# A new written-out order for a five-engine kernel, with one planned duration set from 0.345 to 0.42

## The chip, the cores and the metric

One NeuronCore of a Trainium2 chip (trn2) runs the whole kernel. Its engines are TensorE (PE for matmuls, PEld for its weight loads), VectorE (DVE), ScalarE (ACT), GpSimd (POOL) and SyncE (SP), which issues nearly all DMA transfers. The metric is the device time of one execution in microseconds; smaller is better.

## The reference

Two attentions over the same input `x` (2048 tokens of 512 values) are mixed by a gate.

```python
x = A_x
g = _sigmoid((x * gate_w).sum(-1, keepdims=True))
a = _A_ref(x, A_mem0, A_Wq, A_Wk, A_Wv, A_Wo, A_seg_len)   # recurrent memory, 64 segments
b = _B_ref(x, B_wq, B_wk, B_wv, B_wo, B_beta)              # 4 segments, 32 heads of 16
return g * a + (1 - g) * b
```

The first one is a recurrence. A segment has 8 memory rows and 32 tokens; its output for the memory rows is the memory of the next segment:

```python
for s in range(n_seg):                        # 64 segments of 32 tokens
    h = jnp.concatenate([mem, xs], axis=1)    # 40 rows of 512
    q, k, v = (einsum('btd,dhe->bhte', h, W) for W in (Wq, Wk, Wv))   # 32 heads of 128
    p = softmax(where(mask, q k^T * scale, -1e9))
    o = einsum('bhte,hed->btd', p v, Wo)
    mem = o[:, :M, :]
    outs.append(o[:, M:, :])
```

The second one is an attention within four stretches of 512 tokens, plus a running memory of `phi(k)^T v` over the stretches. It has no recurrence from token to token and so fills the waits of the first.

## The kernel before, in words

The program records some 6,800 operations, each with an engine (or two engines to choose from), what it reads and writes, a planned duration `cost` in microseconds and a priority. `Prog.schedule` then plans: it gives PSUM banks, picks engines and forms of matmuls, and lays down the order on each engine. `Prog.emit` writes the instructions in that order, with semaphore waits for what an operation reads. Each engine works through its own list strictly in order.

In this kernel the order isn't chosen by the planner's priorities. It is written out: the string `ORDER` (lines 15 to 80) holds, for each of the five engines, the sequence of operations, and `sequences()` unpacks it. Where an operation may go to two engines, the list in which it stands decides. With `ORDER` given, the planned durations still set the planned times, and by these the planner gives PSUM banks and orders waits.

```python
words = [a | b << 8 for a, b in zip(raw, raw[len(raw) // 2:])]
for e in self.ENGS:
    ...
    for w in words[at + 1:at + 1 + n]:
        prev += 1 + (w - 65536 if w > 32767 else w)
        out[e].append(self.all[prev])
```

One segment `s` of the first attention (`p_seg`) goes through these steps, for two halves `r` of 16 heads. TensorE's 128 columns are mostly used as four quarters of 32, so that four matmuls with 32-column weights run side by side.

- `k`, `q`, `v`: projections of the 32 rows `hT` (24 tokens and 8 memory rows), line 1422. Each is evicted from PSUM by ScalarE or VectorE (line 1002); k and q are then turned by VectorE (line 1497).
- `H` (line 1029) writes the mask into PSUM, `S` (lines 1512 and 1516) adds the scores, and ScalarE takes the exponential `exp` (line 1521) into `PT`.
- `U` (line 1536): TensorE sums the columns of `PT`. ScalarE takes `ln` (line 1540) and `rc`, the exponential of its negative (line 1542). VectorE multiplies: `nrm` (line 1544). A smaller multiplication `nrr` (line 1546) goes to VectorE or GpSimd.
- `PV` (line 1577) and `PW` (line 1586): probabilities times values, into four PSUM banks, evicted as `OT` by ScalarE or VectorE (line 1002).
- `wo` (line 1314): the output projection. VectorE turns its memory rows, two copies swap blocks, and `hm` (line 1337) writes the memory rows of the next segment's `hT`.

Around these stand the work for the eight rows of each segment that are not on the recurrence (`rk`, `rq`, `rv`, `wor`, done for four segments at once), the second attention (`bL`, its scores, line 1146; `bE`, exponentials, line 1164; `bM`, masks on GpSimd, line 1170; `bPV`, line 1187; `bout`) and the final rows (`brow`, `fin`).

The one planned duration that the change touches stands at line 1545, in `p_u`, which also holds `U`, `ln`, `rc` and `nrr`:

Of the kernel before, what the change touches and what calls it, by code (L numbers as in the profile page):

```python
# [19 lines left out]
    "jybi^^oj}%>U%zo>Jb8OZ<N}L1(=#JDDoS_`pkgh2B0%=U>r|~rbo`cqusO2TW~0a<WCe1=<RUh>xlYGAT@awnt*sMpDAF5er(SIgaCr*VEC!Gp!1GiZ{)5^AJm?7j_+?@1XVC66"  # L20
    "fK}v0dtnjOMt8&ES#TM#+-5CV24f)gF^mT=dd2_h7_tMPi`R}>Q*C+|IKc{F8M+b*CahBw{|@l86F&Jw<gJA$VEhbw5jb2flMdk9=>lxN@wK9KSIXHo05@sWTy_w|B0V@xG|X$k!"
    "5Qc(z>l4d0gO{L*8zySK|+AI=Yc|?i|A>-rv~5b&x$60G`~bF5g;`*UeUgp8#$P~WuO<H3;HrU6qp@?poi!G*1ZFJdo>Z@TR5FXf;4NkN4_;Q_>=tEN6g`@fLb1bpaQZOiBXA>+V"
    "H_fUo0j7tZRV`qWIE%l9QVe4i}WBen=dJJ$-3R$`vD)ECd(}i!6v}wbKMbU|KIybFj0I<yVs21`WWjcz74CIxX<zN6}V_>`=sknfI7Lom-iDQqlY4j3tj35S_u#NIL8@#(|@(^gD"
    "q0MO1`W<fvwgK|q|<WpWYQIAZErNVb+NA!hN)%6Z)m)oCLd#K2<P`G#<>Spirme1+>R!DTrEufjoS2e3LBmW(FSix)!Cv_)X{<k$nW+{BAwE4V<Gi@XNJ6qu-J|I%D~`W1pX(dr6"
    "(Zsdy$M1J#|UcaIjK_A87OP!BGmm~3{MiDW2`b1JS#zG4zYL8z&jn!$w&VgMtAR!PCfvr_vXm#I&D5^58Xr!WX?sD?;Wsu1EGvETU^t@Rm^QJ;WnomV`C2^nywC;mQ$Yfy?Ur|D_"
    "+x^7LIRr4fPb(%|7#Kycye@;J*805BKVblW2D^Y*GHwNd0uQboqwdro;&<wLP(!K-hDODb5;6!@=<%CuNDROMkMxyQ!@7G&;`g2uwoqyYIK2&-U4g}V{#iBP3SzT(=$yDIx0r};d"
    "Nfrr`}5L`NyOOQqQPFs*-F9YE_D=Av!#v~1t^1;Pt@?xMDN{1dK?MP(&QfgfDlfp4L48({ACl!_Z={bdSQl?kBP9gHeF!YDiZ}!fSaJ`F@)>OoG{{7l9QCr;5++xqT}nYJ(f%ef~"
    "c~)u+~#VO0>bU0*1m<2xW-kOk04bH`epzFFYc_HvHD-Ka11iv=>z?H<I=tQX?Qxb~61n`atq8hKl#IxN?r?i*2q4HEG5LAY^gk%flVv+w|Ack1N&eV+-P*$I%~$fqC(V=2F6+_tK"
    "`$8cX!18sAl7csb{#;Jk*=Paxt!Za1~P%cZhXN^zu1U15uA4^8D0gNtMmY~^4ON{QNWB&IM|jnZ6*Xhn-kCz4tQhr7rk=C+VQPuR<@C=B(ynW-%49~@;K9!UNyT@S$JF#tytozt5"
    "C5q%x@h_(LpPy`V@*Acw6w7TY-iq_!{C<tnj^Sg(%r<~diL6o##{=@EL37^jN263L+F9ox%n6xg^Gt&DDu=FUTEBz%LVBu$V;StF#Po6I_Sl#@!P^<e$H^}ZKKyE(N>>^7aeuavs"  # L30
    "k{{#SP{$7ig0u5Y#H#>}Wt<&{zDiRhT?0mtAHBEmPeKPL;WPxrHfu(gCf6ag`T(LL?1@J_fS6ROGaBXcH@L-8_<H^ipOtaX;r-0nFvbWeghvU(DST1;KExcXR$dh9w3HG@%d90<&"
    "ZW<b$c$)3=>3m_l&*Y%8{2^}?JvWB^OX~U;fkSdIUfR$4m;v2B`Bx%y#9>54MH3xB7MT$<H0T`m}T6&coXW6Tz;aqV#X!tpSC9S7t)}gBN}W{riGy>zgB*<TzR7uy-}OUuQyyO)-"
    "siOn$h@AL#ivGJ0EhjT1YoyYvW@MFLY>wp|);&Ib8AT;<D}gmu1TFWeRi2Xv>GoU=hpKt%IM&zyT+LjSMg{%J4pXZF;3H(_mrLFQqV+Mk!eItZb1NzWE}MK`K&_YyvM`A%AvKzYV"
    "6M0H<G6fTl+~AFZw|9zwo$KKdS=2?!i51O%%Fm0IS_mN~K|<SP-X20y3A9NgotFGgo9z#&ED)b^)HyWPWZdZABn)#r-7Kv>_;>|+c47YjIdg`vPoNGMcK=SH8l(t6$@=uwE7Cp>8"
    "J4G5f9fY3Gsdp_1c|2}SxF2o#+IoO!z`7&Dd$OV5rg4fas^_$65>v`>`tO75lLm)1OSd4-&iXHX_h^bH?qYv@SS-tpTj8@=i{0!Fx@dx;B>^y*$&Ibf2aaey?M-8ZvZ+2K906G;w"
    "WHuyZ#$|TBj5~wi3Yz~Vw*NjLKy;YPcpls)v}Wj_Jww``O8;rn?AhSbTfj}M4%p7)QNd<#1yT{P@4!jC%?t&m@28UsI&1?}pF;uNPRSB&F4OJ+^+iK~Symw&j*0|(Ke%>FY#=)BN"
    "0spfp&%?Kz=B6z9)ysf+03461+@^^-o}?i&M^U}c-C+77cFah+fy~TfT9r3H41Qh_k%GH?u0wY8qIIZc3Da0hh!jwt)LdMEzr%qwFd=0Yf$sPLpEI?83~L)1Ja1Ir4Am7O(Z5i7H"
    "sQrz;oYifr9W2n9Nw<l2@YM>RO+vTNqYiL!3<xQL)MTck{vq0&;jvo<Gh^0@8rGT41v2z;L1?*n+3d2;pr7mOweE(dIlIws*&e8XG)n-JF5!io%L><BK7Hv&ktcHjy~mb#d?~jV!"
    "hHj}G5V!QGw)64V9AOABTQzYPI(_@{P9>#MSPW`ymLx8jZ+ez)#j6d+sV=8A(zM$#eqPWZlF9-{?1D%y77{uvWcu*Wk2=1nIHIxroS<Q3gq^AiCitVL6|%S*}&loDNz?@|#Ovrg7"
    "tVs-B{y-BQ})dBi8M82qy(AlnBfoa~TlvstPHxaIbt8p>sJ>DE0b{9e41Ft?THB#-==UG!__3IXK+mmE1QP(Vx{pH-D1WKNm@Fcc2U4-G+QC{ppooCOXH7RU|H$SZ$i`v6)H=-7b"  # L40
    "VYu9TE#oa2e;Z&jsaRW&V{)EovUA||DA8f|LP&=Ln{Y%?&x_<KQD;2W0SBf{m_LaM<h6(5pzs2C2JQ12AqAhbglp-*#);na7n|lyhXr4N4HEHLgWwPD#SSD!HVDR{8{Tu6y*US{T"
    "kwLx);kMarJ>-i{{Z3k#8<PtesK_jfMBE~8$sYcJX(AOU-e^=7McSr$ZHXiS};|I!wb9Pdqj^{>_L5m!wW)1Ls6Lb%H0O&)dMxW-~+*eaNMm3PL2ezgRlUCx~tOTlSM@YAZOAy(+"
    "z^dU-Z??&t7;^!!dagxF)QSuheG>mt@P{{&6k&yP1Anj1uhzysfLXqOsecGwI$Kd#-IvuRHeD@OQnTYhdUyFp@WD)?z{RsFYnxlhNo;lcTNY6C1fJ96$HrHx0|rXq`8t&3>?OYX?"
    "<)v4CH<205=bz9qa^@ie%`w2z&>@rdipAA1>}Y<sNaEnKu|7!KOjkIQ_`aOA`+2z);0%UvJ+8~U&==D!`yqx>Z^gP?-f8^WGLRxBJYiwogJsIWS%SPX(jZ_m)f`L?y(R5c1SxjAF"
    "em3A((TYd)g<DKgO4K}3}ggy+(tB<TAIIyr_ivBEgIMqG7`|tZV8~Nw9D~(7yxX?66;Pox<=z@QIw_#p%1sPj_sQLbL4t`I7jDfJ_Z8&ptNO=pV37awgBQ*N`wG}1~GOjj$hb(@x"
    "$L$wMgZv5_=6w(3`p8ws<7k`RxA?wD+K|&itkvnWA-iuO*&o67enCHF?^!q*%58Z1OtOy7fU|ejn+1Dczju7PY33VEZbgYEJY~*<8jquiU0IN@um83IuqEc;fV9~lbWf`VqK&)Wm"
    "@~|T_g<pj2L%-x!C1<pcE^eLHa#6l!5o)a|8f)IZe0_I*B$SjT>DXlfrGOT6Un`zj+c|WkZq92lVI-X?FktNt3M_87S^#sd~n-hT=Dtxk;_RShz%LNchAa`N5NyA-ii47OK#CbjE"
    "4Rc^wok2GbtuAle8~)ID=&y0*D2I*$(JxvpV<c=QYQ<4LMV6CJM-jDZSOqaN@tjO^FD;T4yG=+*XVo7hj_Jsxx99+TA-Oq<sF@XIoYD%>=UYnHDCl>A8##$O79wD6U_|6HbL$lY)"
    "S+undQd2qO6_jog+ZyNH7X6Sog?C!dI=2Pkl1KD5Wikt?t`I+f<+{ntJs*MsKn${?xgeze#OBK1p$Y84|uV=_#Ue~D%h>OFlQU_Ey*&XzU+-hz>jXE^Uix-A&Fr=~#1b49^Jh$ZB"
    "Kj3fJ@+zZ6kmx~U+wPRvFpyWP1U{ofqun~D`&-jOX!<z3!3Fz{j=<AVtzRDBfac~gS&et0pZaR>l_PUYFY0QSs{%Y$07~WG4=}=;-Nj8(vvuTS#-)wPnpQZHPiQHq>dsF0v*66`$"  # L50
    "81>sk!f}o4=bK;Vih@c{_TEkYK(+s%9xsqdfk*h>+efG&@G)9Cb3sM|ByQTA7#@gc%@N^J;~-8?#`T0Lo%$1vTLwZs&QgZSQ{RpY`Y6R#VSYEYZqj_YZflnF*tB*qiP>jM1v76Lx"
    "E0K`Z#2O-8y9gratC7)%HIur>2P_oH=a5yYQkI;n?VCiEI!?xR{q1S1Ny>01x@Z%OiXc3SV99w9Ex1ok02W&F&$f`osM!Wg6KOHpZqKX7=?>w%-6eOCfSAKok<17?w1P)`fgwR$O"
    "OidduJj~x$o(-yYpW(YG}hZ1SQBsGeG8i?(EC<)WH$&EZ#B^F0=#KIRvhU+i`mD-JdS&pVnU<ev@8sI$U`0Hu3RNGCp5lw!B>5^PH|(F4V5>B1tBS4tKQUb5GF4xmyy)en0m6C^L"
    "3jNYXx8H0~D?+{Dl5Ha}~S>29C%0>$E!NaA?Z-`0R)fMug{-@4h5ApMmSGO65-&=YXcWh49lUDIhYBAoUXO_3paJq+FegHrGO`@W##8=s^L&mYI@_a~fvd~%@<MRqwtTGCrvW#O4"
    "OcF`k%HyT{u9nIsrQ5e;~PQ#rOa}d2jwI}WvyZB=-5PAKlORlF}Jx#rRC-;hxR}h-Kl8g|LU+a~_)f*d2&0=oXoEXlq_ib83)dwy~gctF=X+>6#aOCY~u`A_W07v>I@2ep=-2H&O"
    "=q`ZX0fB@gMUu=D-MM_eR)vKo5;%7?{$a@DFo6324GBNw_8=3q#fdCUAJsOwF0?PQo^3@FX)Mp`gV7N&4jpLm`KC8qU~7}@aF!!8IJqhNr)B<d=E?lIoevt;&dJ@-=MutYoo%5HJ"
    "DeLSX4~&_Vfn2b{J;5Soz5<u>3~MTrsUtsHjMb?)0Z|9YlV<Qo3EViGI>tUcl`93**pH7xO30Ljwk!Zgyl~?b*|HQ$2yIins55)xcJMHYq|Mv?i!o2Vr0we^YI0gH0aWqLm#dkoW"
    "G>ehE{c68@f8n)OngA7P3|~yT0J3;ZrhF_VimlrQ@~_+m9!Gcu~^e55>5IdaHv?`%br;un@)LUM7C_ieI}Vn3oT)Uguu7?xPd4VDyr8Th^TH^Q!)6YErY53lp-E?({S7jsLLldOL"
    "VtZpxfLVeXJR2_sf!^c>qT!qn;fz_^S}KU~aCXwW2P#PZ{Wg_eChF!skwO$RsX7jJs^oqi2gF4^=>Oy;h{E{A&7PFpz{-rP%qJ#6%w-6G>szJ;4ZkH>_q|6wD)>|CF1iCw-qhyU1"
# [1588 lines left out]
```

## Time and profile before

| | |
|---|---|
| Median of 3 runs | 812.8 us (812.7 to 814.73) |
| The profiled execution | 813.89 us, its span 811.9 us |
| TensorE busy | 788.2 us, 97% of the span |
| VectorE, ScalarE, GpSimd busy | 643.7, 523.1, 257.8 us |
| HBM | 30.33 MB read, 8.87 MB written |

The span runs from the first to the last instruction of the program; the time of an execution holds also what lies around it. An engine is busy while one of its instructions runs; for TensorE these are the matmuls, and PEld counts its weight loads. A wait is put down to the instruction that ended it.

### The profile page before, as it was taken

To read this page: it belongs to the slowest core of one execution; us is meant where nothing else is said; L and a number is where in the kernel's file an instruction comes from. 1 tells how busy PE (TensorE), PEld (TensorE's weight loads), DVE (VectorE), ACT (ScalarE), POOL (GpSimd) and SP (SyncE) were. 2 spreads that over 40 slices of the span, in tenths; PEclk is the share of its full clock that TensorE was granted. 3 is DMA by queue.
4 is the path that set the end of the run, shared out by engine and by line. 5 is a ranking of instruction groups with operands and counts; after the bars stand their busy time and mean duration, and the time that the engine had idled before them with its cause. 6 is when DMAs were issued, how large, how long until landed. Compare 5 with 4: busy or idle time off the path is not lost.

```text
span 811.9 us, 51762 instructions
## 1 busy us (share of the span) xinstructions
PE 788.2 (97%) x23598; PEld 501.2 (62%) x23607; DVE 643.7 (79%) x1681; ACT 523.1 (64%) x1198; POOL 257.8 (32%) x564
## 2 busy tenths in 40 slices
...
PEclk9999999999999999999999999999999999999999
...
GB/s 327 417 256 63 47 16 45 36 52 27 48 25 21 46 27 40 33 46 34 21 33 48 38 25 42 30 24 20 40 48 31 21 31 21 16 25 22 22 21 37
DMA packets 71696, 45.14 MB, mean 56 GB/s; under 512 B 50046, under 2 KB 69942, under 8 KB 69942
## 3 DMA queue, kind: packets, MB, share of 16 engines
...
q14 instruction: 33, 0.27, 0.1%
HBM read 30.33 MB, written 8.87 MB: 48 GB/s over the span
## 4 chain that ended last, share of the span: by engine, by line
PE 84%; DVE 8%; DMA 3%; ACT 2%; issue 2%; SPq 1%; POOL 1%; DVEq 0%; POOLq 0%; ACTq 0%
PE pb L1422 46%; PE pb L1314 18%; PE pb L1029 6%; PE pb L1146 3%; PE pb L1187 2%; PE pb L1577 2%; DMA st<-in_gate_w_dram 2%; PE pb L1512 2%; PE pb L1536 1%; PE pb L1031 1%; DVE V_sb L1002 1%; PE pb L1586 1%; DVE st L1002 1%; PE pb L1235 1%; DVE QT_sb L1497 1%
## 5 line engine op out<-in xcount | busy, mean ns | idle before, releaser
L1164 ACT ACTIVATE PTB<-pb 128x640 bf16<-128x640 f32 x240 | 158.5, 705 | 41.0 <-PE pb L1146 29.8
L1002 ACT ACTIVATE st<-pb 128x512 bf16<-128x512 f32 (+2 forms) x232 | 112.9, 499 | 104.3 <-PE pb L1422 76.1
L1422 PE MATMUL pb<-Wv_sb,hT 128*32 128x512 bf16 x2048 | 152.5, 380 | 0.0
L1422 PE MATMUL pb<-Wq_sb,hT 128*32 128x256 bf16 (+1 forms) x3072 | 139.2, 308 | 0.3
L1314 PE MATMUL pb<-Wo_sb,OT_sb 128*32 128x256 bf16 x4096 | 130.8, 273 | 2.2 <-issue 1.8
L1422 PE MATMUL pb<-Wk_sb,hT 128*32 128x512 bf16 x2048 | 131.1, 379 | 1.2 <-issue 0.9
L1314 PEld LDWEIGHTS pb<-Wo_sb,OT_sb 128*32 128x32 bf16 x4096 | 102.3, 96 | 12.6 <-issue 2.3
L1170 POOL TENSOR_SCALAR_AFFINE_SELECT PTB<-PTB 128x512 bf16<-128x512 bf16 x120 | 77.7, 648 | 90.2 <-ACT PTB L1164 82.2
L1422 PEld LDWEIGHTS pb<-Wq_sb,hT 128*32 128x32 bf16 x3072 | 79.7, 97 | 42.4 <-DVE hT L1337 4.4
L1546 POOL TENSOR_TENSOR PT_sb<-PT_sb,rc_sb 128x64 bf16<-128x64 bf16 x81 | 28.9, 356 | 188.9 <-ACT rc_sb L1542 174.9
L1422 PEld LDWEIGHTS pb<-Wk_sb,hT 128*32 128x32 bf16 x2048 | 53.2, 97 | 49.6 <-DVE hT L1337 2.3
L1002 DVE CAST st<-pb 128x512 bf16<-128x512 f32 (+1 forms) x123 | 67.2, 549 | 15.4 <-PE pb L1422 12.7
L1002 ACT ACTIVATE OT_sb<-pb 128x320 bf16<-128x320 f32 (+1 forms) x139 | 57.4, 429 | 32.2 <-PE pb L1586 31.3
L1002 DVE CAST OT_sb<-pb 128x320 bf16<-128x320 f32 (+2 forms) x121 | 56.5, 475 | 18.5 <-PE pb L1586 17.6
L1002 DVE CAST V_sb<-pb 128x512 bf16<-128x512 f32 x90 | 61.5, 684 | 8.8 <-PE pb L1422 7.9
L1497 DVE STREAM_TRANSPOSE QT_sb<-st 128x128 f32<-128x128 f32 (+1 forms) x192 | 61.8, 335 | 8.3 <-ACT st L1002 6.4
L1540 ACT ACTIVATE rc_sb<-pb 128x160 f32<-128x160 f32 x128 | 38.9, 304 | 42.7 <-PE pb L1536 36.2
L1332 DVE STREAM_TRANSPOSE pb<-pb 128x256 f32<-128x256 f32 x63 | 29.3, 465 | 40.7 <-PE pb L1314 40.4
L1521 ACT ACTIVATE PT_sb<-pb 128x224 bf16<-128x224 f32 x128 | 45.5, 356 | 23.0 <-PE pb L1516 19.1
L1422 PEld LDWEIGHTS pb<-Wv_sb,hT 128*32 128x32 bf16 x2048 | 48.0, 97 | 20.0 <-ACT st L1002 0.7
L1497 DVE STREAM_TRANSPOSE KT_sb<-st 128x256 f32<-128x256 f32 x128 | 54.6, 427 | 7.0 <-ACT st L1002 5.5
L1544 DVE TENSOR_TENSOR PT_sb<-PT_sb,rc_sb 128x160 bf16<-128x160 bf16 x128 | 45.2, 353 | 8.9 <-ACT rc_sb L1542 7.3
...
## 6 DMA issues: line engine op xcount, KB each, us to landing
Wv_sb<-in_A_Wv_dram SPq DMA_DIRECT2D x4, 1024.0 KB, 11.2
...
```

Of the source, the lines that this page charges most:

```text
L1002: self.P.op(("act", "dve"), (lambda a: a.activation(dst, src(), ACT.Copy), lambda d: d.tensor_copy(dst, src())), reads=reads, writes=write ...
L1029: ins = pe.matmul(out[32 * c:32 * c + 32], lhsT[:, 32 * c:32 * c + 32], rhs, start=start, stop=stop, tile_position=(0, 32 * c), **kw)
L1164: P.op("act", (lambda dst=dst, src=src: lambda a: a.activation(dst, src(), ACT.Exp, scale=0.25))(), reads=[pair], writes=["%s%d_%d" % (nam ...
L1170: P.op("gp", (lambda pt=pt, ii=ii: (lambda g: g.affine_select(pt, pt, ([[0, len(ii)]] if len(ii) > 1 else []) + [[1, 128]], ALU.is_ge, 0.0 ...
L1314: ins = pe.matmul(pb[so.b][p0:p0 + 32, 0:256], tok(r, g, l), half(h, d, q), start=(r == 0 and g == 0 and l < 2), stop=(r == 1 and g == 3 a ...
L1332: P.op("dve", lambda d: d.transpose(pb[so.b][:, 256:512], pb[so.b][:, 0:256]), reads=[so], writes=[rt], name="turn%s" % name, cost=0.468, ...
L1422: ins = pe.matmul(self.pb[sl.b][32 * g:32 * g + 32, 0:hi - lo], x[:, c, 0:32], cols, start=(c == 0), stop=(c == C - 1), tile_position=(0, ...
L1497: op("dve", (lambda dst=dst, src=src: lambda d: d.transpose(dst, src))(), reads=["st%d%s" % (i, tag)], writes=["%sT%d%s" % (kind, r, tag)] ...
L1521: op("act", lambda a: a.activation(PT[:, r, :], pb[rb.b][:, 0:224], ACT.Exp, scale=SCALE), reads=[rb], writes=["PT%d" % r, "PT%dr" % r], n ...
L1540: op("act", lambda a: a.activation(rc[:, r, :], pb[rb.b][:, 0:160], ACT.Ln), reads=[rb], writes=[rr], name="ln%d_%d" % (s, r), cost=t_act( ...
L1544: op("dve", lambda d: d.tensor_tensor(mine[r], mine[r], by_head(rc[:, r, :]), ALU.mult), reads=[rp, rr], writes=[rp], name="nrm%d_%d" % (s ...
L1546: op(("dve", "gp"), tuple((lambda e: e.tensor_tensor(rest[r], rest[r], late(rc[:, r, :]), ALU.mult)) for _ in range(2)), reads=[rp + "r", rr],
```

## The change

The string `ORDER` is replaced by another one, which holds the same operations. In `p_u` the planned duration of `nrm` goes from 0.345 to 0.42. Nothing else is changed: the operations, their operands, buffers and transfers are the same. SP's list is the same row for row; the lists of TensorE, VectorE, ScalarE and GpSimd differ nearly throughout by moves of a few places, and some operations change between two possible engines (ScalarE's list has 1209 operations instead of 1203, VectorE's 1669 instead of 1681, GpSimd's 566 instead of 560).

```diff
 ORDER = (
-    "c-nPZ2|yIp8~@(U?#`aDpc0BE%HfgsomYk;kY(l-rCDN{VwqNIYMyCore%1Rnn!rynSz9h;(Z%lq-kEEsR;@!3(U@&|9i8?yczhf!tTy|^S$r*eZTK}Pd5Y_F;`It7Qt!M>jdXFZ"
...
+    "c-nPZ2Vm1y6TWBJk-Re4gfbJthOp@XS|DYQ9}1=Hh83VdC}oEkprI59BTz=6Y$$;aAf)V3_J$_xpV88m6(COHB(|RZdy;KQc7B6hTRPpl@!fa#9^Gt(LYKusg5CKRqnI_zFn78kL"
...
 )
...
             op("dve", lambda d: d.tensor_tensor(mine[r], mine[r], by_head(rc[:, r, :]), ALU.mult), reads=[rp, rr],
-               writes=[rp], name="nrm%d_%d" % (s, r), cost=0.345, prio=prio)
+               writes=[rp], name="nrm%d_%d" % (s, r), cost=0.42, prio=prio)
```

More of the change, by code (lines that the diff above doesn't have):

```diff
@@ L20 @@
[L20 to L59, printed above, removed]
@@ new lines @@
+    "7+K{fB@<2ejfeTK7e8OJ_N95|NeZ~?fgcNS(z`mTH(j*iNVeZQ>U5dO|84KcP79J)4Z|iw_r^DseN8=nKct)qX*dU&W>yw_A8vT%*nL?IPSvL=#u=C^Nzu}V9qncf#xO0*X{sa3j"
+    "y}ti(gO|0Gw9S9~G?yh1Q&IdtJtl+qq^=grvkxaEGs+YstM`e{;WT<(I+mHN$|Mcu?g5<U>%T+hKW#k5+bZwf=w)#50D-GNL`L{n4h*@K<oY$&vPO3f{a^ckPh1QSBWkn+L(N_gc"
+    "*v55OP&2-xd4$QiT&4H_Zx*4HFB4`$8^ea#!h2D3Zc9KUo4f}Jq!5sHKIS`~5sasxP<E^;ZO?2z38GGF3Vls5p>`mYNPL^R67-^E_Z(mxk>*j~hoCXurOUWO2-0o>fJ>PfR*a0zm"
+    "Rm|OrsQM{jh<XS!xc~{6=G{fdVGXS-&9pi$d85^$w1bJ+juoHU1&R$Q?iyW~#Y_j4)a6!vc@ctDSG=i_;Kg<Y-zRJX}1Kg}_J2Oq>Lf)E$Y$GuL(2SZHmd9n`=?AAOsqU4Bg<mzk"
@@ new lines @@
+    "0M;DAWPi=so>YEo;kY}+ExBL=%R(3fTc5)O)slMv&CYgtNjT=<lmvTrm=kir3SjwsHDpcPs4D&q-)nN=p2*Lc90G5Ozhx1!x`2akX1btX$KiQC*_f(#;oOD^BKNqC!}i96O0#Szn"
+    "0*Uc=3Klo3a<PPFivA~_uWx<P?x!&fa9$BX7O<;_%|x**Gjdo)w_X~xL|9UcB;ucxVV1!pEP22g}tx`6=a3G;WY@(e=DwR4^aE-@v!iGlc}nF!|IS(BNHB?k0B0Q!;@g<vp^uYU`"
+    "`OTK{n%)T>#yaCc(xA7-WZN5{%g(@UI2K>Mu{!M^%V_C{T4SUySyD3wD+f;>n+TZzluXu4dW%DO`gLh*Oa9=R0!j9L{$EdWp7tF$A(Xzzka43>)a&>aAy0#mi=`c)n1{Mjm1sLh{"
+    "KhfNv%wFcDsrV@6wuxq!LkG#eZn$K>Z(Q$|{IRzSSZDSX}f@L2gq2wxP-LsJC45Zt%R-wbZ-KvkDfpe0LN%1BwbV*HZ$*)tYfM2-{fPQeN9?~ZaBqAwXB+iqE~8Zu!~^OG=1)jkJ"
@@ new lines @@
+    "~HNw#RC|aEaYl#6fy$e#0>{rxc=%yNc16sI$hjs*CR;Ms?Hd08?Yl}VG<Cj-s3HH(8vRyQp_}8J%!Z2eN@DHjO;7$~(+?5@tYODxJ4^~4MmJm^bg)tQk3nqf4Y6i^OA!FMsyZY*|"
+    "^8lBz==lPVp>hR5YdGzKZ+?XvY8_vJO}FR5#x%Zw5PP}5$^qOi=7b!C?6$YeQ0JZw6%?%Z{1L_PVmv;Ngc!yVVFi#E?8@!*dwwoFi96o%Vxu$Q%)sThGxbMW$@<eF$BM?JB2N$#4"
+    "@P*)tTDQb+hgloh9sD-nvH4M($|FX_3{rw(q1UXH`fFW;B?#;RroGo8dvO=BP??j&lgs{7l~OKnl0dkJuqVB0NKkGqwucv9py1ISHSVS!^r0g&S5+9neuyeldwM5WY1AcItgCZe;"
+    "j%52V!=jC2xvjNefOZ25>VBb-^nrqalh5Rqr+e7)3Y|{wM^}n`6Nhg5Z!D$PFS3C4|U!@9)4KundGPh2h>(x?7di5{Ign!Xy_ggpYDM%gL#IQ{gv2c0sfAYz0WPPJtwkLlA{57-N"
```

74 lines of the change are left out of this document (51 added, 23 removed).

## The prediction

> **What bounds the kernel now.** I read the page's head and its chain first, to see which engine sets the end.
>
> ```profile
> span 811.9 us, 51762 instructions
> PE 788.2 (97%) x23598; PEld 501.2 (62%) x23607; DVE 643.7 (79%) x1681; ACT 523.1 (64%) x1198; POOL 257.8 (32%) x564
> PEclk9999999999999999999999999999999999999999
> PE 84%; DVE 8%; DMA 3%; ACT 2%; issue 2%; SPq 1%; POOL 1%; DVEq 0%; POOLq 0%; ACTq 0%
> ```
>
> TensorE is busy for 97% and carries 84% of the chain, at a full clock in every slice. VectorE comes second with 79%. So an order of the same work can move only what TensorE waits. The windows show where that is.
>
> ```profile
> 0.00:60.00 60.00, 54.31 (x989) 27.34 (x998) 39.74 (x105) 34.53 (x67) 29.28 (x77) 1.00 0.93 338
> 460.00:560.00 100.00, 96.82 (x2992) 63.01 (x2984) 78.57 (x216) 66.62 (x153) 28.30 (x60) 1.00 0.12 30
> 760.00:812.00 52.00, 44.95 (x1392) 29.24 (x1384) 39.98 (x106) 25.61 (x63) 14.66 (x30) 1.00 0.10 27
> sum 812.00, PE 788.18 PEld 501.23 DVE 643.65 ACT 523.14 POOL 257.83; mean PE 87.58 PEld 55.69 DVE 71.52 ACT 58.13 POOL 28.65
> ```
>
> The third number of a row is TensorE's busy time. It is idle for 812.00 - 788.18 = 23.8 us: 5.7 in the first 60 us, 7.1 in the last 52, and 11 in the 700 between, of which 3.2 lie in the worst hundred shown. The first stretch keeps the DMA engines 93% busy at 338 GB/s with the weights. The list of SP's transfers is the same, row for row, in the new order, so I count nothing there.
>
> Then the waits, since they name the hand-overs. A row gives total, times and longest. PEld is the weight loader, which runs ahead of the matmuls: its idle time is an upper bound of what a wait cost, the idle time of PE itself a lower one.
>
> ```profile
> PEld pb L1536 <- ACT PT_sb L1521: 9.3, 40, 0.4
> PEld pb L1577 <- DVE PT_sb L1544: 5.1, 16, 0.8
> PEld pb L1512 <- DVE QT_sb L1497: 3.7, 13, 0.5
> PE pb L1314 <- issue: 2.9, 3, 1.1
> PEld pb L1577 <- DVE PT_sb L1546: 2.4, 7, 0.4
> PEld pb L1314 <- ACT OT_sb L1002: 1.4, 6, 0.3
> PEld pb L1187 <- POOL PTB L1170: 1.3, 2, 0.7
> PE pb L1577 <- DVE PT_sb L1544: 1.1, 3, 0.7
> PEld pb L1314 <- DVE OT_sb L1002: 1.0, 4, 0.3
> PE pb L1187 <- POOL PTB L1170: 0.5, 2, 0.4
> PE pb L1314 <- DVE OT_sb L1002: 0.3, 1, 0.3
> ```
>
> The values matmuls PV (L1577) wait for the normalisation nrm (L1544): between 1.1 us (PE) and 1.1 + 5.1 = 6.2. That is the wait which the changed constant names.
>
> **The constant.** It does no work on the chip: the multiplication stays one instruction. How long it really takes:
>
> ```profile
> L1544 DVE TENSOR_TENSOR PT_sb<-PT_sb,rc_sb x128: 261/326/792, 52.1 to 804.6; 128x160 bf16<-128x160 bf16 x128
> L1544 DVE TENSOR_TENSOR PT_sb<-PT_sb,rc_sb 128x160 bf16<-128x160 bf16 x128 | 45.2, 353 | 8.9 <-ACT rc_sb L1542 7.3
> ```
>
> Median 326 ns, mean 353, longest 792. The old 0.345 was the mean; 0.42 lets the planner keep room for the long ones.
>
> **What the change moves.** Engine by engine the two orders hold the same operations. The 128 pairs of sums and values are there in both. What differs is (1) what TensorE is given between a hand-over's two ends, and (2) who does the operations that may go to two engines. I counted both in the two orders, and priced them by rows.
>
> (2) first. ScalarE gets more evictions and VectorE 12 operations fewer (1681 to 1669); 9 of the small normalisations nrr (L1546) leave VectorE for GpSimd.
>
> ```profile
> L1002 ACT ACTIVATE st<-pb 128x512 bf16<-128x512 f32 x126 | 75.2, 598 | 69.2 <-PE pb L1422 65.8 <-PE pb L1029 2.4
> L1546 POOL TENSOR_TENSOR PT_sb<-PT_sb,rc_sb 128x64 bf16<-128x64 bf16 x81 | 28.9, 356 | 188.9 <-ACT rc_sb L1542 174.9 <-PE pb L1422 7.0 <-PE pb L1516 3.7
> L1546 DVE TENSOR_TENSOR PT_sb<-PT_sb,rc_sb 128x64 bf16<-128x64 bf16 x47 | 11.3, 240 | 0.4 <-ACT rc_sb L1542 0.3
> ```
>
> Some 6 operations more of 0.6 us on ScalarE (64% busy) and 12 fewer on VectorE (79%) set no end: both have idle time, and TensorE's matmuls hide them. I take 0; where they stand right ahead of a hand-over is a rival below. A small normalisation costs 356 - 240 = 0.12 us more on GpSimd; nine times that is 1.0 us at most, hidden behind the PV matmuls that go before its reader. I take 0.
>
> Nor does the matmul work change. About a dozen groups go from four quarter-width matmuls to one of full width, or back. By these rows 16 whole ones take 4.1 us, 0.26 each, and 24 quarters, six groups, 1.8 us, 0.30 each; so 0, at most 0.5 us.
>
> ```profile
> L1031 PE MATMUL pb<-xT,Wo_sb 128*128 128x512 bf16 x16 | 4.1, 379 | 0.3 <-issue 0.3
> L1029 PE MATMUL pb<-xT,Wo_sb 128*32 128x512 bf16 x24 | 1.8, 379 | 0.0
> ```
>
> (1) is the sum. A hand-over needs a certain time from the first matmul of its maker to the first of its reader. TensorE has cover for it: the matmuls that stand between the two, each at its pace. The chain in order of time gives the pace, 0.65 us for 12 (0.22 for four) of the projections, 0.87 for 32 of Wo, 0.10 for the 16 scores or the 8 sums.
>
> ```profile
> 411.35 0.65 PE pb L1422 x12
> 412.28 0.10 PE pb L1536 x8
> 412.60 0.10 PE pb L1512 x16
> 416.74 0.87 PE pb L1314 x32
> ```
>
> The need of U -> ln -> rc -> nrm -> PV, from the timeline:
>
> ```profile
> 399.91 0.27 PE L1536 MATMUL pb<-PT_sb,ones_sb 128*32 128x160 bf16 x8
> 400.26 0.30 ACT L1540 ACTIVATE rc_sb<-pb 128x160 f32<-128x160 f32 x1 [0.30 <-PE pb L1536]
> 400.60 0.34 ACT L1542 ACTIVATE rc_sb<-rc_sb 128x160 f32<-128x160 f32 x1
> 331.72 0.33 DVE L1544 TENSOR_TENSOR PT_sb<-PT_sb,rc_sb 128x160 bf16<-128x160 bf16 x1
> 332.11 0.27 PE L1577 MATMUL pb<-PT_sb,V_sb 32*128 32x40 bf16 x16 [0.17 <-DVE PT_sb L1544]
> ```
>
> From U's start to the logarithm 0.35, that 0.30, the gap 0.04, the reciprocal 0.34, then some 0.03, 0.33 and 0.06 (332.11 - 332.05): 1.45 us if nothing stands in the queues. A normalisation that shares its time with GpSimd takes longer (below), so I also count with 1.57.
>
> - **PV.** The middle cover of the 128 rises from 1.77 to 1.88 us. Below 1.45 lie 9 instead of 12, below 1.57 lie 12 instead of 17; the missing time below 1.57 sums to 2.4 us instead of 3.1, a quarter less. A quarter of the wait of 1.1 to 6.2 us is 0.3 to 1.5 us; nearer PE's own row, since the missing time is 3.1: -0.7.
> - **U.** The sums wait for the exponential (L1521), which needs 0.83 us from S: 400.73 to 401.15, its 0.36, and 0.04. The cover of S -> U gives way: below 0.83 lie 14 instead of 11, and the missing time goes from 0.5 to 1.2 us. Between 0 (PE shows no wait there) and a rise of the loader's 9.3 us in the ratio below 1.0 us, 4.5 to 5.6, a quarter or 2.3: I take the missing time itself, +0.7.
>
> ```profile
> 400.73 0.27 PE L1512 MATMUL pb<-QT_sb,KT_sb 128*32 128x40 bf16 x16
> 401.15 0.36 ACT L1521 ACTIVATE PT_sb<-pb 128x224 bf16<-128x224 f32 x1 [0.21 <-PE pb L1516]
> ```
>
> - **wo.** The output projection reads OT 0.88 us after PW starts (an eviction of 0.43 on ScalarE or 0.49 on VectorE with its two hand-overs). 30 covers instead of 22 lie below that, missing 3.1 us instead of 2.2, two fifths more. On waits of 0.3 (PE) to 2.4 us (1.4 + 1.0): 0.1 to 1.0, taken +0.5.
> - **S.** The last half of q has 23 covers below 1.7 us instead of 17, missing 2.7 instead of 1.9. On the loader's 3.7 us two fifths is 1.6, the lower end 0: taken +0.3.
> - **bPV.** Three readings of the other attention's probabilities lacked cover, 2.0 us together; one does now, 0.4. The rows show 0.5 (PE) to 1.8 us (0.5 + 1.3) for GpSimd's masks: 0 to -1.3, taken -1.0.
>
> Sum: -0.7 + 0.7 + 0.5 + 0.3 - 1.0 = -0.2 us. With all lower ends -1.5 + 0 + 0.1 + 0 - 1.3 = -2.7, with all upper ones -0.3 + 2.3 + 1.0 + 1.6 + 0 = +4.6. What PV gains the other hand-overs pay for: TensorE's list has only so many matmuls to stand in the gaps.
>
> The profiled execution took 813.89 us, its span 811.9 and 2.0 around it; that is 1.1 above the median of 812.8. So 813.89 - 0.2 = 813.7 for such an execution, and **812.6 us** for the median.
>
> **A rule against the change.** The long normalisations come with GpSimd at work:
>
> ```profile
> 250.40 0.73 POOL L1244 TENSOR_TENSOR orow<-adot,t_sb 128x256 bf16<-128x256 f32 x1
> 250.51 0.79 DVE L1544 TENSOR_TENSOR PT_sb<-PT_sb,rc_sb 128x160 bf16<-128x160 bf16 x1
> ```
>
> Here nrm took 0.79 us, 0.46 above the median, inside a GpSimd instruction. Nine more nrr on GpSimd start with their nrm, after the same reciprocal. If each adds 0.12, what 0.42 stands above the usual 0.3, that is 1.1 us at most, all on PV's path; then the sum is +0.9 instead of -0.2, inside the same case. [...]
>
> **Rivals.**
>
> *Faster: the cover decides* (0.26). PV's waits end all but for PE's three worst: of the 6.2 us some 3 to 4 go, since the missing time below 1.8 us falls from 11.2 to 9.6 and queues reach that far. With bPV's 1.3 that is about -4.3: 808.5 us. For it speaks that nrm heads the loader's second row; against it, that only 1.1 us shows on PE itself.
>
> *Slower: ScalarE's queue ahead of the exponential* (0.22). In the new order 26 instead of 19 exponentials stand right behind a K eviction. If the eviction is late, exp starts late, U, ln and PV with it. Seven times 0.6 us (the row of 598 ns) is +4.2: 817.0 us. It decides once S -> U has less than 0.83 us, as 14 of 128 have. Against it: ScalarE is idle for a third of the span.
>
> *The gaps that nothing explains* (0.08 that they go, 0.06 that they double). TensorE's queue itself ran dry three times before Wo matmuls, 2.9 us, up to 1.1 each:
>
> ```profile
> 442.38 1.03 PE L1314 MATMUL pb<-Wo_sb,OT_sb 128*32 128x256 bf16 x29 [1.06 <-issue]
> ```
>
> [...]
>
> *The change doesn't do what it says*: the kinds of operation right ahead of nrm are the same (a V eviction 46 and then 49 times, an OT eviction 46 and 45). If PV waits for the queue, not for nrm's length, its row stays at 5.1 and the others add 0.5: 813.3, in the forecast's case.
>
> **How the numbers follow.** About 0.3%, 2.4 us, is what a measurement of this kernel can tell from no change: 810.4 to 815.2. The forecast's case, an even trade, has 0.38 and its own range is 810.1 to 817.4 by the unknown costs, of which I count the part within 2.4 us. Faster is 0.26 + 0.08 = 0.34, slower 0.22 + 0.06 = 0.28. The range for 8 in 10 reaches to both rivals: 808.5 to 817.0.
>
> **What would show it.** Right: TensorE busy within 1 us of 788; the PV <- nrm row falls from 5.1 to about 4, U <- exp stays near or above 9.3, both wo rows together rise above 2.4. Wrong towards faster: PV's row below 2 with the others unchanged. Wrong towards slower: U <- exp above 11 with PE itself waiting, or a longer nrm (mean over 0.38). A changed first 60 us (5.7 idle) would show that I was wrong to count nothing there.

## The result, and the profile after

The changed kernel takes **817.85 us** in the median of 8 runs (815.24 to 820.78), the kernel before 812.97 us beside it (8 runs, 812.7 to 814.73). The ratio is **1.0046, with an interval from 1.0028 to 1.0064**: slower by about 3.7 us. (The two medians lie further apart, 4.9 us; the text goes by the ratio, which has the interval.) Both are above the range of the prediction (808.5 to 817.0 us). Further runs were made on several chips, on which the kernel before took 811.9 to 815.9 us in the median, so below ratios are compared, not times. Single runs of some kernels, the one before among them, took 985 to 2366 us; the ratios leave them out. The profiled execution of the changed kernel took 820.78 us, its slowest.

The head of its page and the windows, in the form in which those of before stand above (the third number of a window is TensorE's busy time, the last three columns are the granted clock, the busy share of the DMA engines and GB/s):

```profile
span 819.0 us, 51698 instructions
PE 794.9 (97%) x23559; PEld 499.2 (61%) x23559; DVE 645.5 (79%) x1669; ACT 527.3 (64%) x1204; POOL 256.6 (31%) x570
0.00:60.00 60.00, 57.02 (x1010) 27.92 (x1014) 39.43 (x104) 34.63 (x68) 28.85 (x77) 1.00 0.93 338
460.00:560.00 100.00, 98.35 (x2971) 63.95 (x2973) 82.29 (x214) 65.14 (x150) 32.09 (x68) 1.00 0.13 32
760.00:819.00 59.00, 51.78 (x1595) 31.96 (x1583) 48.44 (x125) 28.47 (x70) 18.70 (x40) 1.00 0.10 27
```

TensorE is idle no more than before (819.0 - 794.9 = 24.1 us, before 23.8), but it is busy for 6.7 us more with the same matmuls. A lower clock has a part in that, as will be seen, but not all: the run below with `hx19` moved back has the full clock nearly to its end, and TensorE is busy there for 793.4 us. What the rest is stays open. The waits (total, times, longest) say where to look:

```profile
PEld pb L1536 <- ACT PT_sb L1521: 9.3, 31, 0.7
PEld pb L1512 <- DVE QT_sb L1497: 6.0, 24, 0.5
PEld pb L1512 <- DVE KT_sb L1497: 4.4, 11, 0.8
PE pb L1422 <- DMA out_dram<-stg: 3.6, 2, 2.8
PEld pb L1577 <- DVE PT_sb L1544: 3.5, 10, 0.9
PEld pb L1314 <- DVE OT_sb L1002: 1.8, 6, 0.4
PEld pb L1187 <- POOL PTB L1170: 1.7, 4, 0.8
PE pb L1512 <- DVE KT_sb L1497: 1.7, 5, 0.6
PEld pb L1314 <- ACT OT_sb L1002: 1.1, 5, 0.4
PE pb L1577 <- DVE PT_sb L1544: 1.0, 2, 0.8
PE pb L1314 <- issue: 0.7, 1, 0.7
```

The hand-overs that the prediction priced are all there, and each row has moved by between nothing and some two microseconds. The row that stands out is one that it did not have: TensorE itself waits 2.8 us once for a transfer from `stg` to the output. TensorE's timeline around it, before and after:

```profile
274.56 1.93 PE L1314 MATMUL pb<-Wo_sb,OT_sb 128*32 128x256 bf16 x64
276.30 1.05 PE L1422 MATMUL pb<-Wk_sb,xr 128*32 128x512 bf16 x16
```

```profile
274.79 1.94 PE L1314 MATMUL pb<-Wo_sb,OT_sb 128*32 128x256 bf16 x64
279.57 1.47 PE L1422 MATMUL pb<-Wk_sb,xr 128*32 128x512 bf16 x16 [2.85 <-DMA out_dram<-stg]
280.81 1.93 PE L1422 MATMUL pb<-Wk_sb,hT 128*32 128x512 bf16 x16
```

The rest projection `rk5_1` (Wk times `xr`) follows the output projection at once before; after, it stands for 2.85 us. It waits because its eviction goes to the staging buffer `stg` from which `dma_out3` still stores final rows; the planner here lets the first matmul into a PSUM bank wait for all that the bank's eviction needs. And the 16 matmuls that took 1.05 us take 1.47 and then 1.93. Who issued that store, and when, is in SP's timeline, before and after (start, duration, line, transfer):

```profile
264.93 1.22 SPq L910 DMA_TRANSPOSE xT<-in_A_x_dram  x1
270.65 0.50 SPq L986 DMA_DIRECT2D wqB_sb<-in_B_wq_dram  x1
273.71 0.36 SPq L1291 DMA_DIRECT2D out_dram<-stg  x1
```

```profile
270.08 1.21 SPq L910 DMA_TRANSPOSE xT<-in_A_x_dram  x1
271.34 1.32 SPq L1088 DMA_TRANSPOSE stg<-KT  x1
272.71 0.55 SPq L1613 DMA_DIRECT2D a_rows<-ao  x1
273.30 1.15 SPq L986 DMA_DIRECT2D wvB_sb<-in_B_wv_dram  x1
274.50 0.97 SPq L986 DMA_DIRECT2D wqB_sb<-in_B_wq_dram  x1
275.52 0.51 SPq L1291 DMA_DIRECT2D out_dram<-stg  x1
```

The list is the same (three of the six rows of before are shown). Its first row, the transposed load of x (`dma_x3_0`), comes 5.15 us later, and the five rows behind it are pushed together: the store is issued at 275.52, 1.65 us after `fin3` ended at 273.87, and TensorE goes on 4.05 us after that. Before, it was issued 0.03 us after `fin3` (273.68), and 2.59 us later TensorE went on without a wait (by the trace's semaphore records the store had landed 1.72 us after its issue). GpSimd's timeline says what the load waited for, before and after:

```profile
264.25 0.33 POOL L1219 TENSOR_SCALAR rden<-rden,omgP_sb 128x16 f32<-128x16 f32 x1 [1.44 <-DVE rden L1224]
264.64 0.26 POOL L1468 COPY hT<-xT 128x96 bf16<-128x96 bf16 x1
```

```profile
264.06 0.33 POOL L1219 TENSOR_SCALAR rden<-rden,omgP_sb 128x16 f32<-128x16 f32 x1 [1.24 <-DVE rden L1224]
268.70 0.33 POOL L1219 TENSOR_SCALAR rmem<-rmem,gP_sb 128x16 f32<-128x16 f32 x1 [4.31 <-DVE rmem L1242]
269.11 0.62 POOL L1221 TENSOR_TENSOR t_sb<-t_sb,rmem 128x256 f32<-128x256 f32 x1
269.80 0.26 POOL L1468 COPY hT<-xT 128x96 bf16<-128x96 bf16 x1
```

`hx19` (L1468) is the last reader of the old contents of `xT`. Before, it stood right behind `bgad6`. Now it stands behind `bgam6` and `bam6`, and `bgam6` waits 4.31 us for VectorE's `rmem`.

The granted clock in three windows behind the wait:

```profile
279.00:281.00 2.00, 1.43 (x20) 0.68 (x24) 0.00 (x0) 0.00 (x0) 0.00 (x0) 0.77 0.00 1
281.00:283.00 2.00, 2.00 (x28) 0.74 (x20) 1.23 (x3) 1.41 (x3) 0.00 (x0) 0.50 0.00 0
283.00:285.00 2.00, 2.00 (x48) 1.19 (x44) 0.90 (x3) 0.98 (x2) 0.00 (x0) 0.88 0.06 16
```

The middle window lies at half throughout. If what is missing in the others is half clock too, it lasted (0.23 + 0.50 + 0.12) x 2 / 0.5 = 3.4 us; the trace's own record of the clock has it at 0.50 from 280.07 to 283.48, and sixteen matmuls that otherwise take 1.05 us took 1.93 in it. Ahead of it TensorE had stood for 2.85 us.

### The profile page after: what moved, and what is told of

It is laid out like the page before. It is cut to its first block, busy times and chain, and to the rows that moved or that the text cites. A ratio compares the mean times of both kernels' runs of the same rounds, so it can differ in the third digit from the quotient of the medians.

```text
span 819.0 us, 51698 instructions
## 1 busy us (share of the span) xinstructions
PE 794.9 (97%) x23559; PEld 499.2 (61%) x23559; DVE 645.5 (79%) x1669; ACT 527.3 (64%) x1204; POOL 256.6 (31%) x570
## 4 chain that ended last, share of the span: by engine, by line
PE 81%; DVE 8%; DMA 4%; ACT 3%; issue 2%; POOL 1%; SPq 1%; DVEq 0%; ACTq 0%; POOLq 0%
PE pb L1422 45%; PE pb L1314 16%; PE pb L1029 5%; PE pb L1146 3%; PE pb L1577 2%; DMA Wv_sb<-in_A_Wv_dram 2%; PE pb L1512 2%; PE pb L1187 2%; PE pb L1536 2%; PE pb L1031 1%; DVE st L1002 1%; DMA out_dram<-stg 1%; ACT PTB L1164 1%; PE pb L1586 1%; DVE QT_sb L1497 1%
## 5 line engine op out<-in xcount | busy, mean ns | idle before, releaser
L1002 ACT ACTIVATE st<-pb 128x512 bf16<-128x512 f32 (+2 forms) x245 | 122.4, 512 | 109.5 <-PE pb L1422 87.0
L1422 PE MATMUL pb<-Wv_sb,hT 128*32 128x512 bf16 x2048 | 154.8, 380 | 0.1
L1422 PE MATMUL pb<-Wq_sb,hT 128*32 128x512 bf16 (+1 forms) x3072 | 143.4, 309 | 1.1 <-DVE hT L1337 0.6
L1546 POOL TENSOR_TENSOR PT_sb<-PT_sb,rc_sb 128x64 bf16<-128x64 bf16 x90 | 31.8, 353 | 180.1 <-ACT rc_sb L1542 178.8
L1002 ACT ACTIVATE OT_sb<-pb 128x320 bf16<-128x320 f32 (+1 forms) x145 | 60.2, 429 | 41.3 <-PE pb L1586 38.8
L1002 DVE CAST OT_sb<-pb 128x320 bf16<-128x320 f32 (+2 forms) x115 | 54.1, 474 | 19.7 <-PE pb L1586 18.4
L1002 DVE CAST V_sb<-pb 128x512 bf16<-128x512 f32 x84 | 57.6, 685 | 8.9 <-PE pb L1422 7.2
L1544 DVE TENSOR_TENSOR PT_sb<-PT_sb,rc_sb 128x160 bf16<-128x160 bf16 x128 | 45.2, 353 | 15.6 <-ACT rc_sb L1542 14.3
L1002 DVE CAST st<-pb 128x256 bf16<-128x256 f32 (+1 forms) x96 | 50.5, 532 | 8.3 <-PE pb L1422 7.1
## 6 DMA issues: line engine op xcount, KB each, us to landing
Wq_sb<-in_A_Wq_dram SPq DMA_DIRECT2D x4, 1024.0 KB, 27.4
```

The lines of the kernel that those rows point to most:

```text
L1002: self.P.op(("act", "dve"), (lambda a: a.activation(dst, src(), ACT.Copy), lambda d: d.tensor_copy(dst, src())), reads=reads, writes=write ...
L1422: ins = pe.matmul(self.pb[sl.b][32 * g:32 * g + 32, 0:hi - lo], x[:, c, 0:32], cols, start=(c == 0), stop=(c == C - 1), tile_position=(0, ...
L1544: op("dve", lambda d: d.tensor_tensor(mine[r], mine[r], by_head(rc[:, r, :]), ALU.mult), reads=[rp, rr], writes=[rp], name="nrm%d_%d" % (s ...
L1546: op(("dve", "gp"), tuple((lambda e: e.tensor_tensor(rest[r], rest[r], late(rc[:, r, :]), ALU.mult)) for _ in range(2)), reads=[rp + "r", rr],
```

## The experiments

Theory A: SP's order carried GpSimd's delay to the store, and the store's delay to TensorE. Theory B: the loss is spread, mostly over the waits at S, where VectorE turns k and q late. A change of one place in a list is written below as a diff of that list. The edits add lines to the program, so line numbers in rows of these runs are higher (by 10 with a single move, by 45 in the run with fifteen moves).

**hx19 moved back, and moved late in the kernel before**

```diff
 GpSimd, new order:  bgad6
+hx19
 bgam6, bam6
-hx19
 bo6
```

> The new order with one move: on GpSimd's list hx19 goes back from behind bgam6 and bam6 to right behind bgad6, where it stood before. Everything else, PSUM banks included, is as in the new order. Theory A (SP is held): the transposed load of x into xT waits for hx19, and SP issues in order, so the store dma_out3 behind it came late and TensorE stood 3.0 us at rk5_1, then ran some 3 us at half clock. Then the load is issued near 265 us instead of 270.1, rk5_1 waits under 0.5 us, the granted clock is 1.0, and the time falls by 3.0 to 4.4 us, from 817.9 to 813.5 to 814.9. Theory B (the loss is spread: S waits for the turned k and q behind other work in VectorE's queue, +4.3 us over the profile): the wait of 3.0 us goes but other waits take its place, and the time falls by less than 1 us, to 817 or above.

Measured: **1.0001 (0.9990 to 1.0012)**. The load is issued at 269.18 (everything lies some 4 us later here from the start on), the store 0.03 us after `fin3`:

```profile
269.18 1.22 SPq L920 DMA_TRANSPOSE xT<-in_A_x_dram  x1
277.71 0.36 SPq L1301 DMA_DIRECT2D out_dram<-stg  x1
```

`rk5_1` follows at its usual spacing and the clock stays at 1.00. The reverse in the old order:

```diff
 GpSimd, old order:  bgad6
-hx19
 bad6, qr18, bgam6, bo6
+hx19
 OTr17
```

> The kernel before with the reverse move alone: hx19 goes on GpSimd's list from right behind bgad6 to behind bgam6 and bo6, so that it should end near 270.0 us, as in the new order, and the transposed load of x, with dma_out3 behind it, be issued 5 us later. Theory A: TensorE waits at rk5_1 for the store by 2 to 3 us, its clock dips after it, and the time goes from 813.0 to 815.5 to 817.4. Theory B: the wait shows, but under 1 us of it reaches the end: 813 to 814.

Measured: **1.0042 (1.0018 to 1.0066)**. The one operation brings in a loss of the same size:

```profile
PE pb L1432 <- DMA out_dram<-stg: 3.2, 2, 2.6
271.08 1.22 SPq L920 DMA_TRANSPOSE xT<-in_A_x_dram  x1
276.03 0.51 SPq L1301 DMA_DIRECT2D out_dram<-stg  x1
```

Theory A holds in both directions. A dose between the two, in the old order:

```diff
-hx19
 bad6, qr18, bgam6
+hx19
 bo6, OTr17
```

> The kernel before with hx19 moved only behind bgam6, not behind bo6 as well: it ends near 268.4 us instead of 264.9 or 271.0. The 5.4 us of SP's issues behind it then end about when fin3 does (273.7), so the store is issued at 273.9 at most. Theory A with a threshold: 3.5 us of lateness cost nothing or under 0.5 us (ratio 0.999 to 1.001), while the 6 us of the other run cost 3.4 us. If the loss grows in proportion to the lateness, the ratio is 1.002 to 1.003.

Measured: 1.0005 (0.9987 to 1.0023). In its trace the load is issued at 269.81, the store 0.02 us after `fin3` (274.99), and TensorE does not wait. The five issues that SP still has to make ahead of the store (269.81 to 275.01) just fit in. So the traces show a threshold, not a proportion: issued 5.18 us ahead of the end of `fin3` (8.75 before), the load cost TensorE no wait, and 3.79 us ahead of it (270.08 and 273.87, in the changed kernel) one of 2.85 us. The ratio alone does not decide it, since its interval reaches into the 1.002 to 1.003 of a proportion.

**The order of SP alone**

```diff
 SP, new order:
-dma_x3_0
 bkn7, ast17, dma_wvB8, dma_wqB9, dma_out3
+dma_x3_0
```

> The new order with one move on SP's list: the transposed load of x (dma_x3_0, line 910) goes from ahead of bkn7, ast17, dma_wvB8, dma_wqB9 and dma_out3 to right behind dma_out3. GpSimd's list stays as in the new order, so hx19 is as late as there. Theory A (what holds the store is SP's order, not hx19 itself): dma_out3 is issued when fin3 ends, near 274 us, TensorE does not wait at rk5_1, the clock stays at 1.0 around 282 us, and the ratio to before falls from 1.0046 to 1.000 to 1.002, as with hx19 moved back. Rival C (it is the load of x and its traffic beside the store that costs, or the late hx19 by another way): the wait shrinks by half at most and the ratio stays above 1.003.

Measured: **1.0013 (0.9997 to 1.0030)**. `hx19` is as late as in the new order (270.85), and the store is issued when `fin3` ends (274.65):

```profile
274.68 0.36 SPq L1301 DMA_DIRECT2D out_dram<-stg  x1
275.08 1.20 SPq L920 DMA_TRANSPOSE xT<-in_A_x_dram  x1
PE 789.4 (97%) x23548; PEld 500.9 (62%) x23559; DVE 645.5 (79%) x1669; ACT 527.4 (65%) x1204; POOL 258.1 (32%) x570
```

The second part of the wait, the store's 4.05 us, was tried with the weight slices:

```diff
 SP, new order:  dma_x3_0, bkn7, ast17
-dma_wvB8, dma_wqB9
 dma_out3
+dma_wvB8, dma_wqB9
```

> The new order with another move on SP's list: the two slices of weights (dma_wvB8 and dma_wqB9, 2.1 us of issue together) go behind dma_out3; the transposed load, bkn7 and ast17 stay ahead of it and are as late as in the new order. The store is then issued when fin3 ends (about 273.9 instead of 275.5) behind 3.1 us of late issues. If only the lateness of its issue counts, the wait at rk5_1 falls from 3.0 to about 1.4 us; if the traffic of the slices slowed the store too (it took 4.0 us to land, where before it took at most 2.6), the wait falls under 0.5 us. Either way no half clock follows, and the ratio falls to 1.001 to 1.003.

Measured: 1.0025 (1.0009 to 1.0040). The store is issued at 274.87 (`fin3` 274.84), and `rk5_1` runs 2.65 us later at its usual spacing, although the load of x and `bkn7` are late:

```profile
274.87 0.34 SPq L1302 DMA_DIRECT2D out_dram<-stg  x1
277.52 1.04 PE L1433 MATMUL pb<-Wk_sb,xr 128*32 128x512 bf16 x16
```

So the slices ahead of it delayed the store's issue. That their traffic also slowed its landing, as was expected, the traces do not bear out. By their semaphore records the store lands in sixteen parts. In the changed kernel fifteen have landed at 277.81, 2.29 us after the issue; the sixteenth comes at 279.53, and TensorE goes on at 279.57. The eight packets of that last part begin at 278.37, just where a packet of 16 KB on the page's `instruction` queue ends (277.02 to 278.39). The four other executions with the late store (`hx19` late in the old order, the matmuls added, the moves on VectorE's list, and 0.345) show the same: fifteen parts by 2.2 to 2.3 us, the last at 3.6 to 4.1, its packets beginning within 0.02 us of the end of such a packet. In before, in the dose and in the three versions that cure the store, no such packet is under way while the store's data move, and all sixteen parts land in 1.7 to 2.0 us, in the dose right behind the same two slices. The execution of before has 185 of these packets for TensorE's 47,205 matmuls and weight loads, 255 for each, so I take them for TensorE's own code (an estimate). Some 1.7 of the 2.85 us are thus an unlucky meeting of the late store with such a packet, shown by the traces alone; no run moved the packet.

**The clock**

```diff
 TensorE, new order:  wo18_7
+keep0 ... keep11   (4 matmuls each, Wk with itself, into rk5_1's bank; nobody reads them)
 rk5_1
```

> The new order, hx19 late as in it, with twelve operations added on TensorE's list right ahead of rk5_1 (48 matmuls into a bank that nobody reads, 2.6 us at the usual 0.22 us each; PSUM banks of all else as in the new order). TensorE works instead of standing while the store is on its way, so only the clock can change. If the half clock after the wait costs 1.0 to 1.7 us of the loss, it is granted 1.00 around 282 us, k19, q19 and v19 stand at their usual spacing, and the ratio falls from 1.0046 to about 1.003. If the clock's dip is not from the pause, it is still 0.5 there and the ratio stays at 1.0045 or more.

Measured: 1.0050 (1.0034 to 1.0066), so the ratio did not fall as theory A expected. The clock did as expected:

```profile
279.00:281.00 2.00, 2.00 (x44) 0.94 (x38) 0.00 (x0) 0.59 (x2) 0.00 (x0) 1.00 0.00 0
281.00:283.00 2.00, 2.00 (x51) 1.18 (x44) 1.89 (x5) 1.69 (x4) 0.00 (x0) 1.00 0.03 8
283.00:285.00 2.00, 2.00 (x72) 1.35 (x68) 1.40 (x5) 1.14 (x3) 0.00 (x0) 1.00 0.06 16
```

`rk5_1` starts at 279.33, as late as without the added matmuls, but at full clock; the two segments around the wait take 25.5 us instead of 27.7 (table below). So here the pause brought the half clock (0.50 with it, 1.00 without, from 281 to 283 us), and in the execution that had it the half clock cost some 2 us (27.7 against 25.5, one execution each). Not every run has it: of the eight runs of the changed kernel four have a mean granted clock of 1.000 over the whole run and take 816.6 us in the mean, three have 0.997 or 0.998 and take 819.8. (A half clock of 3.4 us lowers the mean by 0.5 x 3.4 / 819 = 0.002. The eighth run, with 0.999, can't be told: the execution with the matmuls added has 0.999 too, by a half clock in its last 1.1 us.) With the matmuls added, six runs lie within 816.5 to 817.9, where the eight go from 815.2 to 820.8. That the ratio did not fall is within the two intervals; what share of the loss the clock has stays open.

**The waits at S**

```diff
 VectorE, new order, e.g.:
-row5
 kev6_0, qtp6_0, ktp6_0
+row5
```

> The new order with fifteen moves on VectorE's list alone: at the segments where S waited most in its profile (6, 7, 17, 20, 22, 24, 27, 31, 34, 40, 54, 55, 60) an operation that nobody waits for soon (row, bmzr, bphiq, par, t1) goes from ahead of the turning of k to right behind it. PSUM banks are held to those of the new order. Theory B: S waited 5.9 us in all in the new order's profile and 1.7 before; with 0.42 us less in the queue at each of these places some 3 us of it go, and the time falls from 817.9 to about 815. Theory A: these waits fall too, but a wait at S is followed by later work that catches up on nothing on TensorE, so the sum should go as well; what tells is the size: if the waits at S were already much smaller in the usual run than in the profiled one, the time falls by under 1 us.

Measured: 1.0066 (1.0051 to 1.0081), no gain. S did wait less for KT, 0.9 us at the loader instead of 4.4, but the mask H now waited for `row` (L1390 here):

```profile
PE pb L1074 <- DVE ao L1390: 1.4, 2, 0.7
PEld pb L1557 <- DVE QT_sb L1542: 6.8, 21, 1.0
PEld pb L1557 <- DVE KT_sb L1542: 0.9, 4, 0.3
```

`row` reads the bank of the output projection, and in the held plan H takes that bank next; so `row` was not work that can stand behind. With the banks left to the plan, `hx19` moved back and two more moves:

> The new order with hx19 moved back, as in the run that gave 1.0001, and the moves on VectorE's list that put the turning of k ahead of work that can stand behind it (row, bmzr, bmzu, bphiq, par, t1, bQm), this time with the PSUM banks left to the plan, so that no early bank waits for a delayed row, as H did in the run with the banks held (0.9 us at segments 6 and 22). Theory B: the waits at S fall from 5.8 us to under 3.9 without coming back at H, and the ratio falls to 0.996 to 0.998, faster than both kernels. If the waits at S come back elsewhere again, the ratio stays at 0.999 to 1.002.

Measured: 1.0003 (0.9988 to 1.0018), against 1.0001, 1.0013 and 1.0025 of the three versions that only cure the store. TensorE's own wait at S for turned k and q goes from 1.9 us (1.7 and 0.2) to 1.3; nothing of it can be told in the time. Theory B is not the loss, though a share of under a microsecond would not show.

**The constant**

```diff
-               writes=[rp], name="nrm%d_%d" % (s, r), cost=0.42, prio=prio)
+               writes=[rp], name="nrm%d_%d" % (s, r), cost=0.345, prio=prio)
```

> The new order with the constant put back to 0.345. No engine's list changes, but the planned times do, and by them 327 of TensorE's operations get other PSUM banks, from rk2_1 on to about segment 36. If the bank plan that comes with 0.42 matters, the time differs from 817.9 by more than 1 us either way; if only the order matters (the prediction's view, which counted nothing for the constant), it stays within 1 us of 817.9, with the wait at rk5_1 and the waits at S as they are.

Measured: 1.0033 (1.0019 to 1.0047), with the same wait at `rk5_1` (2.8 us) and nearly the same rows at S. The other banks change nothing that can be told. (In the old order the constant changes neither lists nor banks; fifteen operations only name the same waits in another order.)

**A version from both orders**

From the traces, the time from one segment's first k projection on TensorE to another's, in us (one profiled execution each):

| kernel | start to 18 | 18 to 20 | 20 to 33 | 33 to 53 | 53 to 63 | 63 to end |
|---|---|---|---|---|---|---|
| before | 266.5 | 23.4 | 155.0 | 239.7 | 110.6 | 16.7 |
| before, hx19 late | 267.4 | 27.4 | 154.7 | 239.7 | 110.8 | 16.3 |
| changed | 266.7 | 27.7 | 158.3 | 236.9 | 113.9 | 15.6 |
| changed, hx19 back | 270.7 | 23.3 | 156.0 | 237.2 | 114.1 | 15.5 |
| changed, load behind the store | 267.5 | 23.5 | 154.8 | 237.1 | 113.7 | 15.5 |
| changed, twelve operations added | 266.9 | 25.5 | 157.0 | 236.0 | 113.8 | 15.6 |
| from both orders | 267.7 | 23.4 | 152.8 | 236.8 | 111.8 | 16.2 |

The new order is faster by some 3 us between segments 33 and 53 and slower by as much between 53 and 63, in each of its executions. So the two were put together: old order to segment 32, new order (with the moves of the run that gave 1.0003) to 53, old order from there.

> A version from the traces: the order before until segment 32 (about 440 us on the chip) and from segment 53 on (about 685 us), and between them the new order with the moves of the run that gave 1.0003; hx19 stands where it stood before, and the constant is 0.345. Summing TensorE's excess spacing over four traces with the new order and three with the old, the new order loses 4.3 us up to segment 32 (without the wait for the store), gains 3 us from there to segment 53 and loses 2.7 us after. If such sums add up on the clock, the time is 2 to 3 us under before: 0.996 to 0.998, faster than both kernels. If the seams cost as much (banks, queues and code that each half expects otherwise), or if the gains were gaps of issue that move to other places, the ratio is 0.999 to 1.002.

Measured: **0.9986 (0.9970 to 1.0001)**. Once more, and with one move on TensorE's list beside it:

> The same version without that move, once more beside it on the same chip: its ratio was 0.9986 with an interval from 0.997 to 1.0001. If it is faster than before, as the sums over the traces say, it comes out between 0.9965 and 0.9995 again; if the 1.4 thousandths were chance, at 1.000 or above.

> The version made from both orders, with one move on TensorE's list: k45_0 goes ahead of the rest projection rv12_0, which waited 0.83 us for another output store (dma_out8) while hm44, all that k45_0 needs, had ended 0.7 us before. If the wait is covered now, 0.6 to 0.8 us go, and the ratio to before falls from 0.9986 to about 0.998, below 1.0 with its whole interval. If the hand-over or the evictions behind it give the gain back, the ratio stays with that of the version without the move (0.998 to 1.000).

Measured: **0.9984 (0.9968 to 0.9999)** for the same version, and 0.9990 (0.9976 to 1.0004) with the move. There the wait at `rv12_0` (0.76 us in the version without the move) is gone in the trace, a later rest projection waits 0.52 us for a store in its place, and the time doesn't show it. The version from both orders lies about 1.2 us under the kernel before in both its sets of runs. That is half of what the sums promised, and as one interval just reaches 1.0 and the other just does not, a gain is likely rather than shown.

## Why the prediction was wrong

**The step that failed** is "The list of SP's transfers is the same, row for row, in the new order, so I count nothing there." It was said of the first 60 us, and for the rest of the span the sum has no term for transfers at all. The list was the same; what its rows wait for was not. One row of GpSimd moved behind a wait of 4.31 us, the first of six rows in SP's list waited for it, and the sixth was one that TensorE needed. That is 2.85 us of pause, some 1.7 of it by the unlucky meeting with a 16 KB packet, and in some of the runs a half clock after it: 27.7 instead of 23.4 us for two segments in the profiled execution, and 3.4 to 3.7 us in the ratios (1.0042 by putting it in, 1.0046 against 1.0001 by taking it out). A moved operation counts with every queue that waits for it; I had followed the moves in the engines' own lists alone.

**The sum of the rest** came near. The three versions without the wait lie at 1.0001, 1.0013 and 1.0025, in the mean 1.1 us above before (0.0013 x 813), where the sum was -0.2. TensorE's busy time was to stay within 1 us of 788: it is 794.9 with the half clock, and 789.4, 789.4 and 793.4 in the three versions without, so this sign says little. Its terms, by the same rows:

- PV, taken -0.7: the loader's row falls from 5.1 to 3.5 (16 to 10 times), PE's from 1.1 to 1.0. Right in kind; the gain lies between 0.1 and 1.7.
- The constant, taken 0: right for the lists that were there, and by the run at 0.345 its banks do not matter either. What stood against the change (small normalisations on GpSimd beside nrm, up to +1.1) did not bite: nrm's mean is 353 ns as before.

```profile
L1544 DVE TENSOR_TENSOR PT_sb<-PT_sb,rc_sb 128x160 bf16<-128x160 bf16 x128 | 45.2, 353 | 15.6 <-ACT rc_sb L1542 14.3
```

- U, taken +0.7: the loader's row stays at 9.3, in fewer and longer waits (31, up to 0.7). The rival "ScalarE's queue ahead of the exponential", with a row above 11, is out.
- wo, taken +0.5: 2.4 us at the loader become 2.9 (1.8 + 1.1). Right.
- **S, taken +0.3, is the term that was mis-sized**: 6.2 us at the loader (3.7 + 2.5) become 10.4, and 1.9 show on TensorE itself. I had counted only the matmuls between q and S; what came late beyond that was VectorE's turning, behind `row` and the like in its queue (with those moved behind it, the loader's row for KT fell to 0.9). The row of before for k, and the smaller one of TensorE itself after:

```profile
PEld pb L1512 <- DVE KT_sb L1497: 2.5, 9, 0.5
PE pb L1512 <- DVE QT_sb L1497: 0.2, 1, 0.2
```

- bPV, taken -1.0: the loader's row for GpSimd's masks rises from 1.3 to 1.7. The places did not go: before, the loader waited at `bPV10_1` (0.66) and `bPV15_1` (0.65); after, 0.26 and 0.82 there, and 0.40 at `bPV1_0` and 0.26 at `bPV2_1`. So the cover that I had counted did not tell which readings wait.
- The gaps before Wo matmuls fall from 2.9 to 0.7 us, as the small rival had it; they were not what decided. In the traces the three of before and the one after end 2.4 to 2.7 us after a 16 KB packet of the `instruction` queue began, and these come every 4.1 us in the median. That the packet is their cause, and that a new order should drop or double them, no run shows.
- The idle time of the first 60 us fell from 5.7 to 3.0 us, with the DMA engines as busy as before (0.93), and segment 18 starts 0.2 us later all the same (266.7): TensorE was busier there and no faster. This was to be the sign of a changed first stretch, but it is not one: executions whose first 60 us are those of the old order idle for 5.7, 4.0 and 6.0 us there, and those of the new one for 3.0 to 5.3.

The slower case had 0.28, on another mechanism; the range ended 0.85 us below the measured median.
